# A fused attention-and-MLP kernel rewritten in hand order: q grouped by head, the gate as a column of K, attention gated apart, W3's remainder in column tiles

## The chip, the cores and the metric

The kernel runs on one core of a Trainium2 chip. The time is the device time of one execution, in microseconds (us). "Fast" runs are those in the undisturbed state; every run quoted here is fast, except one single run whose state is unknown and which is marked. TensorE is called PE in the profile, VectorE is DVE, ScalarE is ACT, GpSimd is POOL, and SP is the engine that issues most of the DMA transfers. PEld is the loading of weights into PE, which overlaps with matmuls.

## The reference, cut to what matters

The inputs are bf16: x is 2048 by 640, there are 32 heads of 20 features, and the MLP is 1728 wide.

```
q, k, v = split(x @ wqkv)                 # A: linear attention
phi = where(t > 0, t + 1, exp(t)) + 1e-6
kv  = sum_s phi(k)[s,d] v[s,e]            # per head, 20 x 20
z   = sum_s phi(k)[s,d]                   # per head, 20
a   = ((phi(q) @ kv) / (phi(q) @ z + 1e-6)) @ wo

h   = gelu(layernorm(x) @ w1)             # B: mixer
hs  = (h in four groups of 160 features, shifted by +1, -1, +2, -2 tokens) @ w2
x1  = x + hs
b   = x1 + gelu(layernorm(x1) @ w3) @ w4

g   = sigmoid(sum(x * gate_w))            # one number per token
out = g * a + (1 - g) * b
```

## The kernel before

Tokens come in 16 chunks of 128 or 4 tiles of 512, and features in 5 chunks of 128. kv is never built from v: G = x^T phi(k) is, then kv = wv^T G, and M = kv @ wo, so that attention costs five matmuls per half of an output chunk. A tile framework orders the instructions of each engine by priority. PSUM, where the matmuls write, is handed out as four "pairs" (`pp`), each 128 x 2 x 512 in float32. An engine that still has to read a pair keeps PE from writing into it.

The stages on PE are, in order: K, Q (with the gate), G, then W1 with kv and W2 for the first tile, then four rounds. A round holds W3 of a tile with W2 of the next one, then W4 and the attention product. The parts that the change and the argument touch:

```
    def gate_unit():                      # gate: 5 tiny + 20 column-tiled matmuls
        ...
            nc.tensor.matmul(pt[:, 1, 32 * dc:32 * (dc + 1)], lhsT=gw_row[0:1, ...], rhs=ones32[0:1, :], ...)
        ...
                nc.tensor.matmul(pt[32 * t:32 * (t + 1), 0, :], lhsT=gwb[:, dc, :], rhs=xT[:, dc, ...], ...)

    def z_unit():                         # called after the last G
        ... 32 column-tiled sums over phi(k) ...
        nc.vector.tensor_copy(zv[:, 0], pt[:, :, 0:HD])                            # zz, high part
        nc.vector.tensor_tensor(zv[:, 1], pt[:, :, 0:HD], zv[:, 0], op=ALU.subtract)  # zz, low part
        nc.sync.dma_start_transpose(zT[:], zz[:])
        nc.vector.tensor_reduce(zc[:], zT[:]..., op=ALU.add)                       # needs the transpose
        for j in range(DC):
            nc.vector.tensor_scalar_mul(zbd[:, j, :], hmask[:, j, :], zc[:, j:j + 1])

    def kv_unit(gs):                      # called with (0,1), (2,3), (4,5): three pairs
        pt = pair()
        ... 5 matmuls for each of the six blocks of kv ...
                    nc.vector.tensor_tensor(kvT[0:w, b, ...], pt[0:w, i, ...], mask[...], op=ALU.mult)

    def scale_unit(j, i):                 # 10 times: expand r = g/den to chunk j, scale phi(q)
        pt = pair()
        for t in (2 * i, 2 * i + 1):
            nc.tensor.matmul(pt[:, t % 2, :], lhsT=emat[32 * t:32 * (t + 1), j * P:(j + 1) * P], rhs=r_bf[...], ...)
        nc.vector.tensor_tensor(sl, sl, pt[:], op=ALU.mult)

    def w1_unit(t, fcs):
        ...
                for g in range(4):        # chunk 4 holds the last 32 features of each shift group
                    nc.scalar.activation(hsT[32 * g:32 * (g + 1), 4, o:o + TS], pt[32 * g:32 * (g + 1), i, :],
                                         ACT.Gelu_apprx_tanh)

    def w3_unit(t, fcs):                  # F = 1728 is padded to 14 chunks of 128: the last one is half zeros
        ...
```

## Time and profile before

| kernel before | |
|---|---|
| median of 3 runs | 288.09 us (287.43 to 288.32) |
| span in the profile | 286.1 us |
| PE, DVE, ACT busy | 273.3 us (96%), 132.6 (46%), 92.0 (32%) |

These lines are from the profile page: the busy times, the PE row and the granted PE clock in 40 equal slices (a digit is tenths), the share of each engine in the chain of work that ended last, and the costliest group.

```profile
span 286.1 us, 4181 instructions
PE 273.3 (96%) x1730; PEld 162.2 (57%) x1730; DVE 132.6 (46%) x266; ACT 92.0 (32%) x117; POOL 24.1 (8%) x47
...
PE   6999999999967999999899999999999999999994
...
PEclk9999999999985999999999999999999999999999
...
PE 78%; DVE 8%; DMA 6%; ACT 3%; issue 2%; POOL 1%; DVEq 0%; SPq 0%; ACTq 0%; POOLq 0%
...
L450 PE MATMUL pp<-lnxT,w_sb 128*128 128x512 bf16 x280 | 63.4, 379 | 1.2 <-ACT h_1268 L452 0.8
```

PE is the bound, but the slices twelve and thirteen (about 80 to 93 us) show it at six and seven tenths, and its clock at eight and five tenths. The mean of one matmul in a group (379 ns) overlaps with its neighbours; in a stream ten such 512-column matmuls take 2.16 us, 216 ns each. Next is the table of windows over the stages as PE's order gives them (K, then, after a cut, G, W1 and round 0). The columns are: window, length; busy time of PE, PEld, DVE, ACT and POOL with instructions in brackets; granted clock; DMA share; GB/s.

```profile
0.00:28.80 28.80, 26.25 (x174) 17.58 (x175) 17.74 (x35) 11.85 (x16) 10.15 (x24) 1.00 1.00 276
...
52.15:75.18 23.03, 23.03 (x193) 16.32 (x192) 18.81 (x57) 4.59 (x8) 3.81 (x6) 1.00 0.30 59
75.18:114.45 39.27, 34.19 (x195) 17.13 (x191) 20.93 (x54) 18.86 (x32) 5.08 (x7) 0.87 0.51 115
114.45:164.04 49.59, 48.34 (x304) 28.00 (x303) 25.37 (x36) 17.23 (x22) 1.27 (x2) 1.00 0.10 24
```

The stage from 75.18 us loses time twice: 39.27 − 34.19 = 5.1 us of idle time, and a clock of 0.87. Round 0 is 8.4 us longer than round 1, which takes 41.16 us without a gap. A finer table of windows of the same kernel, same columns, shows where the clock drops, and the waits of PE between 70 and 120 us (total us, times, longest) say for what.

```profile
80.00:85.00 5.00, 2.69 (x27) 2.11 (x26) 2.47 (x5) 3.15 (x6) 0.00 (x0) 0.85 0.24 46
85.00:90.00 5.00, 2.76 (x15) 1.22 (x14) 2.66 (x17) 0.00 (x0) 2.55 (x3) 0.50 0.74 148
90.00:95.00 5.00, 5.00 (x16) 1.94 (x15) 0.00 (x0) 1.09 (x2) 0.00 (x0) 0.63 1.04 368
```

```profile
PE pp L285 <- DVE zz L261: 2.3, 1, 2.3
PE pp L358 <- DVE kvT L293: 2.2, 1, 2.2
```

VectorE's own order in time in this stretch (start us, busy us, line, operation, and the idle time before it with its releaser) says why it was late:

```profile
86.41 0.22 DVE L263 TENSOR_REDUCE zc<-zT 128x5 f32<-128x40 bf16 x1 [3.50 <-DMA zT<-zz]
...
87.36 1.39 DVE L293 TENSOR_TENSOR kvT<-pp,bmask 120x120 bf16<-120x120 f32 x10
```

VectorE takes its instructions in order. It came to `zz`, the z sums, only at 81.24 us, behind rows of layer norm 1, and the first kv pair waited for it (2.3 us). Then it stood at `zc`, which needs the transpose of z, for 3.50 us, and the masking of kv (`kvT`), which needs nothing from z, stood behind it. The three kv pairs stayed full, and PE had no pair to write W1 into.

### The profile page before, as it was taken

The page shows a single profiled execution, that of the slowest core. Times are in us where ns is not written, and L with a number is a line of the kernel's source. Part 1 is how long each engine was busy: PE and PEld are TensorE (multiplying, and loading weights), DVE is VectorE, ACT ScalarE, POOL GpSimd, SP SyncE. Part 2 cuts the span into 40 slices and gives each one's busy share as a digit, 9 for nine tenths or more (in the row PEclk, how much of TensorE's full clock was granted, in tenths as well). Part 3 has the DMA queues.
Part 4 walks back from the last instruction along what each step waited for, and adds up shares of the span by engine and source line. Part 5 has one row for each costly group of instructions (what it writes and reads, how often), then busy time and mean ns, then how long its engine had stood idle before and what let it go on. Part 6 is the DMA issues. An engine that isn't in the chain of part 4 may idle for free.

```text
span 286.1 us, 4181 instructions
## 1 busy us (share of the span) xinstructions
PE 273.3 (96%) x1730; PEld 162.2 (57%) x1730; DVE 132.6 (46%) x266; ACT 92.0 (32%) x117; POOL 24.1 (8%) x47
## 2 busy tenths in 40 slices
PE   6999999999967999999899999999999999999994
PEld 3677444677542543544377655577655577545772
DVE  1588788888733367485625244034252045100121
ACT  1455435311440529732314022404033304143000
POOL 8500100011213010000001000001000010000000
PEclk9999999999985999999999999999999999999999
DMA  8999884025548804000002400003300007100001
GB/s 207 214 318 363 221 269 136 3 40 98 109 79 231 170 0 92 2 0 0 0 2 66 98 23 0 2 23 69 92 2 0 2 23 112 51 0 0 25 32 37
DMA packets 43464, 22.96 MB, mean 80 GB/s; under 512 B 33670, under 2 KB 42375, under 8 KB 43447
## 3 DMA queue, kind: packets, MB, share of 16 engines
q1 hardware_dynamic: 41669, 19.68, 28.1%
q0 software_dynamic: 464, 2.21, 2.3%
q10 hardware_dynamic: 1314, 0.82, 0.9%
q8 instruction: 13, 0.21, 0.3%
q14 instruction: 4, 0.03, 0.0%
HBM read 11.96 MB, written 2.62 MB: 51 GB/s over the span
## 4 chain that ended last, share of the span: by engine, by line
PE 78%; DVE 8%; DMA 6%; ACT 3%; issue 2%; POOL 1%; DVEq 0%; SPq 0%; ACTq 0%; POOLq 0%
PE pp L450 21%; PE pp L463 21%; PE pp L202 8%; PE pp L460 8%; PE pp L212 7%; PE pp L419 6%; DMA lnxT<-ln 4%; PE pp L358 3%; DMA x_sb<-in_A_x_dram 1%; DMA zT<-zz 1%; DVE st1s L185 1%; DVE ln L347 1%; POOL rstd_191 L182 1%; PE pp L303 1%; ACT ln L437 1%
## 5 line engine op out<-in xcount | busy, mean ns | idle before, releaser
L450 PE MATMUL pp<-lnxT,w_sb 128*128 128x512 bf16 x280 | 63.4, 379 | 1.2 <-ACT h_1268 L452 0.8
L450 PEld LDWEIGHTS <-w_sb 128*128 128x128 bf16 x280 | 27.1, 98 | 32.3 <-issue 2.5
L192 ACT ACTIVATE e<-pp 128x640 bf16<-128x640 f32 (+2 forms) x28 | 21.8, 780 | 24.0 <-PE pp L202 14.8
L460 PE MATMUL pp<-m_sb,pqT 128*128 128x320 bf16 x160 | 27.0, 299 | 0.0
L419 PE MATMUL pp<-w_sb,hsT 128*128 128x320 bf16 x160 | 23.9, 299 | 0.0
L202 PE MATMUL pp<-wkq,xT 128*128 128x320 bf16 x160 | 23.1, 308 | 0.0
L358 PE MATMUL pp<-lnxT,w_sb 128*128 128x512 bf16 x80 | 20.8, 422 | 2.2 <-DVE kvT L293 2.2
L212 PE MATMUL pp<-xT,wkq 128*128 128x512 bf16 x100 | 22.1, 379 | 0.0
L273 PE MATMUL pp<-pk,x_sb 128*128 128x320 bf16 x160 | 21.9, 299 | 0.0
L419 PEld LDWEIGHTS <-hsT 128*128 128x128 bf16 x160 | 15.4, 98 | 8.1 <-issue 0.7
L202 PEld LDWEIGHTS <-xT 128*128 128x128 bf16 x160 | 16.1, 101 | 6.7
L460 PEld LDWEIGHTS <-pqT 128*128 128x128 bf16 x160 | 15.7, 98 | 6.7
L273 PEld LDWEIGHTS <-x_sb 128*128 128x128 bf16 x160 | 15.7, 98 | 6.2
L463 PE MATMUL pp<-w_sb,h_1682 128*128 128x320 bf16 x112 | 16.5, 299 | 0.0
L463 PE MATMUL pp<-w_sb,h_2026 128*128 128x320 bf16 x112 | 16.5, 299 | 0.0
L463 PE MATMUL pp<-w_sb,h_2370 128*128 128x320 bf16 x112 | 16.5, 299 | 0.0
L463 PE MATMUL pp<-w_sb,h_1268 128*128 128x320 bf16 x112 | 16.5, 299 | 0.0
L212 PEld LDWEIGHTS <-wkq 128*128 128x128 bf16 x100 | 9.6, 98 | 11.6 <-issue 0.4
L358 PEld LDWEIGHTS <-w_sb 128*128 128x128 bf16 x80 | 8.3, 107 | 13.8 <-issue 4.5
L326 DVE TENSOR_TENSOR pqT<-pqT,pp 128x1024 bf16<-128x1024 bf16 x10 | 12.1, 1217 | 6.4 <-PE pp L323 6.3
L366 ACT ACTIVATE hsT<-pp 128x512 bf16<-128x512 f32 x16 | 8.6, 596 | 18.8 <-PE pp L358 18.8
L194 DVE SCALAR_TENSOR_TENSOR pk<-pp,e 128x640 bf16<-128x640 f32 x16 | 13.2, 825 | 1.7
(197 smaller groups left out, 280.7 us busy)
## 6 DMA issues: line engine op xcount, KB each, us to landing
out_dram<-oc SPq DMA_DIRECT2D x15, 160.0 KB, 2.0
w_sb<-in_B_w_dram SPq DMA_DIRECT2D x1, 2160.0 KB
w_sb<-in_B_w_dram POOLq DMA_DIRECT2D x1, 2080.0 KB, 11.0
x_sb<-in_A_x_dram SPq DMA_DIRECT2D x3, 640.0 KB, 8.5
wkq<-in_A_wqkv_dram SPq DMA_DIRECT2D x2, 800.0 KB, 9.8
wkq<-in_A_wqkv_dram ACTq DMA_DIRECT2D x2, 400.0 KB, 4.8
w_sb<-in_B_w_dram SPq DMA_DIRECT2D x1, 800.0 KB
wo_sb<-in_A_wo_dram SPq DMA_DIRECT2D x5, 150.0 KB, 9.3
```

What stands on the lines that cost most here:

```text
L192: nc.scalar.activation(ev, src, ACT.Exp)
L194: nc.vector.scalar_tensor_tensor(dst, src, 0.0, ev, op0=ALU.max, op1=ALU.add)
L202: nc.tensor.matmul(pt[:, hf, 0:c1 - c0], lhsT=xT[:, dc, cs], rhs=wk_sb[:, dc, c0:c1], start=(dc == 0), stop=(dc == DC - 1))
L212: nc.tensor.matmul(pt[:, i, :], lhsT=wq_sb[:, dc, j * P:(j + 1) * P], rhs=xT[:, dc, ts_], start=(dc == 0), stop=(dc == DC - 1))
L273: nc.tensor.matmul(pt[:, hf, 0:HD], lhsT=x_sb[:, c, fc * P:(fc + 1) * P], rhs=pk[:, c, hf * HD:(hf + 1) * HD], start=(c == 0), stop=(c == ...
L326: nc.vector.tensor_tensor(sl, sl, pt[:], op=ALU.mult)
L358: nc.tensor.matmul(pt[:, i, :], lhsT=w1_sb[:, dc, CG * fc:CG * fc + P], rhs=lnxT[t][:, dc, :], start=(dc == 0), stop=(dc == DC - 1))
L366: nc.scalar.activation(hsT[:, fc, o:o + TS], pt[:, i, :], ACT.Gelu_apprx_tanh)
L419: nc.tensor.matmul(pt[:, hf, 0:HD], lhsT=hsT[:, fc, 2 + c * P:2 + (c + 1) * P], rhs=w2_sb[:, fc, hf * HD:(hf + 1) * HD], start=(fc == 0), ...
L450: nc.tensor.matmul(pt[:, i, :], lhsT=w3_sb[:, dc, fc * P:(fc + 1) * P], rhs=lnT[:, dc, :], start=(dc == 0), stop=(dc == DC - 1))
L460: nc.tensor.matmul(pt[:, hf, 0:HD], lhsT=pqT[:, j, c * P:(c + 1) * P], rhs=m_sb[:, j, hf * HD:(hf + 1) * HD], start=(j == 0), stop=False)
L463: nc.tensor.matmul(pt[:, hf, 0:HD], lhsT=h2[:, fc, cc * P:(cc + 1) * P], rhs=w4_sb[:, fc, hf * HD:(hf + 1) * HD], start=False, stop=(fc == ...
```

## The change

The intent: less PE work, and an order in which PE never waits for a late z. The scheduler is switched off (`manual_schedule`), so each engine runs its instructions as written. The diff is long; this is its core, with cuts marked.

```
+    ctx.enter_context(tc.manual_schedule())
 # q regrouped by head: every chunk j holds 4 of the 20 features of all 32 heads
+        nc.gpsimd.tensor_copy(wq_sb[:, dc, :]...("p (j h i) -> p j h i"), wq_raw[:, dc, :]...("p (h j i) -> p j h i"))
 # so one expansion of r serves all five chunks
-    def scale_unit(j, i): ...                               # 20 matmuls, 10 multiplies from PSUM
+    def r_unit():                                           # 4 matmuls, 2 copies
+    def scale_t(t):                                         # 4 multiplies of 128 x 2560
+        nc.vector.tensor_tensor(sl, sl, rb[:, t:t + 1, :].broadcast_to([P, DC, TS]), op=ALU.mult)
 # the gate is column 641 of K
-    def gate_unit(): ...
+        gq.dma_start(wk_sb[:, :, D:D + 1], gate_w.rearrange("(c p o) -> p c o", p=P, o=1))
+                n = HD + hf                                 # in k_mm: second half has 321 columns
 # K starts on the chunks of wk as they land; z within Q
+    k_mm(kp[0], 0, (0,))
+    x_turn(1)
+    k_mm(kp[0], 0, (1,))
+    ...
+        if n == 1:
+            zp = z_mm()
+        if n == 2:
+            z_evac(zp)
 # all six kv blocks in one pair, M in 32-column tiles
-    kv_unit((0, 1)); kv_unit((2, 3)); kv_unit((4, 5))
+    kv_unit()
+                    nc.tensor.matmul(pt[32 * q:32 * (q + 1), hf, 0:HD], lhsT=kvT[:, 2 * q + p, j, :], ...)
 # one gelu for chunk 4, four copies on VectorE; layer norm 2 on VectorE, scaling of x1 on ScalarE
+                nc.scalar.activation(hx[:, 0:TS], pt[:, i, :], ACT.Gelu_apprx_tanh)
+                for g in range(4):
+                    nc.vector.tensor_copy(hsT[32 * g:32 * (g + 1), 4, o:o + TS], hx[32 * g:32 * (g + 1), 0:TS])
 # attention gated apart from W4, in units of its own between those of W3
+    def att_unit(t, cc):                                    # x1 += gate * (phi(q) @ M)
 # W3's last 64 features: two 64-column tiles of 256 tokens each, in place of 512 columns of half zeros
+                        nc.tensor.matmul(pt[FR * v:FR * (v + 1), k, 0:LT], lhsT=w3_sb[:, dc, FF * P:F],
+                                         rhs=lnT[:, dc, v * LT:(v + 1) * LT], ...)
-    for fcs in w1_split: ... den_unit() ... scale_unit(i - 1, 0) ... m_unit(i)   # den with W1, the rest in round 0
+    g_unit(0); z_fin(); dp = den_mm(); ... r_unit()                              # within G
+    for j in range(DC): m_unit(j)                                                # before W2
```

## The prediction

> **What bounds the kernel now.** TensorE: the page gives PE 96% busy, VectorE 46%, ScalarE 32%; the chain that ended last is 78% PE. In the chain a 512-column matmul streams in 216 ns (30 in 6.47 us), a 320-column one in 136 ns. The last three W3/W4 rounds take 41.2, 41.2 and 35.8 us without a gap; the first takes 49.5 us (114.5 to 164.0), because the r expansions, the M products and short waits sit in it.
>
> The weak stretch is 80 to 95 us (table of windows): PE busy 2.69 and 2.76 us in two 5 us windows, waiting for VectorE (zz 2.3 us, kvT 2.2 us), granted clock 0.85, 0.50, 0.63. So 4.6 us idle and, estimated from the clocks, some 5 us lost at half speed. The Trainium skill (TensorE: Matmul & The Clock Gate, Part 1) says an idle window of about 3.4 us halves the clock; this dip agrees.
>
> **PE work.**
> - r expansion, 20 to 4 matmuls: before, about 0.64 us in each of five W3 steps, now about 0.5 us once: -2.8 us.
> - Gate: 20 column-tiled and 5 tiny matmuls go; a 641st column of K costs nothing: -1.4 us.
> - W3: 280 to 260 full matmuls, plus 40 of 256 columns in two 64-column tiles: -4.3 + 2.2 = -2.1 us. The Trainium skill (TensorEngine Tiling, Theoretical Speedup) promises up to 2x; the trace supports it: 32-column z sums, 32 in 1.27 us (40 ns against 136).
> - M in 32-column tiles, 80 at about 40 ns instead of 20 at 136: +0.5 us.
> - The rest is unchanged. Attention gated apart adds no matmul; it costs 16 VectorE operations of about 0.88 us, in rounds where VectorE is a third busy.
> Sum: -6 us.
>
> **What it moves.** z comes during Q, so its transpose (3.5 us) is done long before W1; kv and M no longer wait for it. That should remove most idle time and the clock dip at 80 to 95 us: -7 to -9 us. The fourfold 32-partition gelu (589 ns each) becomes one ScalarE pass plus copies, which removes gaps of 1 us near 113 us. K starts on chunks of wk as they land: 0 to -1 us.
>
> **New costs.** VectorE is nearly as loaded as PE in the G/W1 stretch: 16 statistics at 1.12 us, a 3.4 us reciprocal, scales and LN, about 28 us against PE's 24 us of G. I expect M to wait for kvT about 1 us. The gate column is a transfer of 640 two-byte pieces that the second K matmul waits for (0 to 1.5 us). The regrouping of wq on GpSimd should finish (24 us) before Q starts (28 us).
>
> **Sum.** Q starts near 28 us (29 before), G near 51 (52), round 0 near 108 (114.5); rounds 40.7, 40.7, 40.7, 35.2 us; tail 3.9. Span about 269, time about 2 us more, and 1 us for waits not foreseen: 272 us, 5.6% less, range 267.5 to 278. Chances: faster by over 2% 0.95, within 2% 0.04, slower 0.01.
>
> **What would show it.** Right: round 0 about 41 us, rounds 1 and 2 half a microsecond shorter, granted clock 1.00 from 75 to 110 us, M's wait under 2 us. Wrong: PE waiting for kvT or hsT near 85 to 95 us with a clock dip (adds 5 us); PE waiting on the gate column at 4 to 7 us or on wq at 28 us; column-tiled W3 not running two at a time (rounds of 41.2 or more).
>
> **What would make it wrong.** VectorE falling behind in the G/W1 stretch: in hand order one late operation delays all behind it.

## The result and the profile after

The kernel took 274.23 us (median of 4 runs, 273.93 to 274.57), against 287.89 us (median of 4 runs, 287.43 to 288.32: the three above and one more) before. The ratio is 0.9518, with a 95% interval of 0.95 to 0.9537. Ratios and intervals are from fast runs alone; they are not quite the ratios of the medians (0.9526 here). The prediction was 272.0 us with a range of 267.5 to 278.

The profile page after, the lines that answer to those of before:

```profile
span 272.4 us, 4350 instructions
PE 264.0 (97%) x1781; PEld 160.3 (59%) x1781; DVE 141.1 (52%) x275; ACT 84.5 (31%) x124; POOL 29.0 (11%) x65
...
PEclk9799999999999999999999999999999999999998
...
PE 94%; DMA 2%; ACT 1%; issue 1%; DVE 0%; ACTq 0%; POOLq 0%
```

The dip of the clock near 85 us has gone and a smaller one has appeared in the second slice. The chain that ended last is now 94% PE, and 2% is one DMA transfer. The stages after (table of windows, columns as before; again K, G, W1 and round 0):

```profile
0.00:32.32 32.32, 27.81 (x187) 18.45 (x188) 17.63 (x34) 12.62 (x31) 9.47 (x32) 0.95 0.98 260
...
55.21:78.68 23.47, 23.47 (x186) 16.03 (x185) 22.64 (x59) 6.21 (x8) 4.06 (x6) 1.00 0.26 43
78.68:110.73 32.05, 31.54 (x252) 17.18 (x250) 25.64 (x60) 15.10 (x26) 10.46 (x17) 1.00 0.64 145
110.73:151.78 41.05, 41.05 (x269) 25.64 (x268) 16.88 (x31) 13.38 (x17) 1.28 (x2) 1.00 0.12 29
```

| stage | before | after | difference |
|---|---|---|---|
| head and K | 28.94 | 32.32 | +3.4 |
| Q | 23.21 | 22.89 | −0.3 |
| G | 23.03 | 23.47 | +0.4 |
| W1, kv, first W2 | 39.27 | 32.05 | −7.2 |
| round 0 | 49.59 | 41.05 | −8.5 |
| rounds 1, 2, 3 | 41.16, 41.20, 35.80 | 40.88, 40.88, 35.46 | −0.9 |
| tail | 3.9 | 3.4 | −0.5 |
| span | 286.1 | 272.4 | −13.7 |

The table starts Q at its first matmul, 28.94 us in the kernel before; the windows further up cut 0.14 us ahead of it. Nearly the whole gain is in the W1 stage and in round 0, and the head gives 3.4 us of it back. G is longer by what moved into it: the denominator (1.26 us) and r (0.40 us) came, the z sums (1.27 us) went to Q. The same finer windows as before, now with a clock of 1.00 throughout (the sum of PE's idle time in these 15 us is 0.5 us):

```profile
80.00:85.00 5.00, 5.00 (x38) 2.76 (x37) 3.97 (x9) 1.28 (x1) 2.85 (x4) 1.00 0.66 131
85.00:90.00 5.00, 4.49 (x34) 2.34 (x32) 2.23 (x8) 3.64 (x7) 3.64 (x7) 1.00 0.34 52
90.00:95.00 5.00, 5.00 (x93) 3.03 (x91) 4.61 (x14) 4.24 (x8) 0.00 (x0) 1.00 0.99 365
```

The W1 stage adds up from these views: 4.6 us of idle time went; the second W1 and kv, which ran at about half clock before, took 7.33 and 2.65 us and now take 4.48 and 1.60 us, so 3.9 us; the denominator (1.26 us) moved into G; and M moved in, for 2.9 us. That is −6.9 us, where −7.2 was measured.

In round 0, a few pieces of the chain of work before, in order of time (start, us, what), show what the r expansions cost; the last two are from round 1, which has none:

```profile
123.16 0.32 PE pp L323 x2
123.48 2.26 PE pp L450 x10
125.75 0.32 PE pp L323 x2
126.07 1.47 PE pp L419 x10
...
135.58 0.32 PE pp L323 x2
135.90 0.98 PE pp L303 x4
...
164.04 2.16 PE pp L450 x10
166.19 1.36 PE pp L419 x10
```

Each pair of r matmuls (L323), 32 rows of PE wide, took 0.32 us. The last two pairs ran as four matmuls at once, as PE's order in time of the same kernel shows:

```profile
139.89 0.39 PE L323 MATMUL pp<-r_bf,emat 32*128 32x512 bf16 x4
```

So the ten pairs took nine such slots, 2.9 us. The full matmuls right after a pair took longer too: ten of W3 2.26 in place of 2.16 us, ten of W2 1.47 in place of 1.36 us. Six groups show this, 0.65 us in all. The five M units took 3.2 us, four of 0.54 or 0.55 us and the last of 0.98 us, where weights of 120 and of 40 rows take turns; they moved to the stage before. With 1.25 us of idle time (49.59 − 48.34), about 0.3 us by which the W3 groups behind the two waits were longer, and 0.3 us for the column tiles, this adds up to 8.6 us, where 8.5 was measured.

The head is where the prediction missed. PE's order in time after, from 5 us, and the wait that goes with it:

```profile
5.40 0.30 PE L199 MATMUL pp<-wk_sb,xT 128*128 128x320 bf16 x1
7.71 0.30 PE L199 MATMUL pp<-wk_sb,xT 128*128 128x321 bf16 x1 [2.01 <-DMA wk_sb<-in_gate_w_dram]
```

The list of DMA issues of that kernel in the first 8 us (what, issuing engine, kind, count, KB, us from issue to landing) has the transfer:

```profile
wk_sb<-in_gate_w_dram POOLq DMA_DIRECT2D x1, 1.2 KB, 6.4
```

The second K matmul is the first with 321 columns, and it waited 2.01 us for the gate column: 1.2 KB in 640 pieces of two bytes, 6.4 us from issue to landing. This trace records the full clock from 4.76 to 8.18 us and half of it from 8.18 to 11.59 us, as the next two windows of the same kernel show. In the second of them PE gets through 11 matmuls in 2 us, where it gets through 17 at full speed (one that straddles an edge counts in both windows).

```profile
8.00:10.00 2.00, 1.94 (x17) 1.36 (x15) 0.68 (x2) 0.00 (x0) 1.37 (x3) 0.54 1.14 227
10.00:12.00 2.00, 2.00 (x11) 1.18 (x9) 0.30 (x1) 0.00 (x0) 0.00 (x0) 0.60 1.03 220
```

### The profile page after: what moved, and what is told of

It is laid out like the page before. It is cut to its first block, busy times and chain, and to the rows that moved or that the text cites. A ratio compares the mean times of both kernels' runs of the same rounds, so it can differ in the third digit from the quotient of the medians.

```text
span 272.4 us, 4350 instructions
## 1 busy us (share of the span) xinstructions
PE 264.0 (97%) x1781; PEld 160.3 (59%) x1781; DVE 141.1 (52%) x275; ACT 84.5 (31%) x124; POOL 29.0 (11%) x65
## 4 chain that ended last, share of the span: by engine, by line
PE 94%; DMA 2%; ACT 1%; issue 1%; DVE 0%; ACTq 0%; POOLq 0%
PE pp L524 22%; PE pp L499 21%; PE pp L347 8%; PE pp L452 8%; PE pp L377 8%; PE pp L483 8%; PE pp L246 8%; PE pp L199 8%; DMA wk_sb<-in_gate_w_dram 2%; PE pp L415 1%; PE pp L504 1%; ACT e L191 1%; PE pp L262 0%; PE pp L285 0%; PE pp L215 0%
## 5 line engine op out<-in xcount | busy, mean ns | idle before, releaser
L524 PE MATMUL pp<-w_sb,h 128*128 128x320 bf16 x448 | 61.5, 299 | 0.0
L507 ACT ACTIVATE h<-pp 128x1024 bf16<-128x1024 f32 (+1 forms) x28 | 27.8, 993 | 103.8 <-PE pp L499 95.5
L524 PEld LDWEIGHTS <-h 128*128 128x128 bf16 x448 | 43.5, 98 | 17.5 <-issue 0.8
L499 PEld LDWEIGHTS <-w_sb 128*128 128x128 bf16 x260 | 25.4, 98 | 26.7
L530 DVE SCALAR_TENSOR_TENSOR oc<-pp,omg,x 128x640 bf16<-128x640 f32 x15 | 13.3, 884 | 44.7 <-PE pp L524 44.7
L486 DVE SCALAR_TENSOR_TENSOR x<-pp,gate,x 128x640 f32<-128x640 f32 x16 | 13.9, 868 | 29.4 <-PE pp L483 29.4
L199 PE MATMUL pp<-wk_sb,xT 128*128 128x320 bf16 (+1 forms) x160 | 23.9, 309 | 2.4 <-DMA wk_sb<-in_gate_w_dram 2.0
L455 DVE TENSOR_TENSOR x<-pp,x_sb 128x640 f32<-128x640 f32 x16 | 13.1, 820 | 23.4 <-PE pp L452 23.4
L191 ACT ACTIVATE e<-pp 128x640 bf16<-128x640 f32 (+1 forms) x26 | 21.2, 830 | 9.3 <-PE pp L246 7.9
L246 PE MATMUL pp<-xT,wq_sb 128*128 128x512 bf16 x100 | 21.9, 379 | 0.0
```

The costliest lines, as they stand in the source:

```text
L191: nc.scalar.activation(ev, src, ACT.Exp)
L199: nc.tensor.matmul(pt[:, hf, 0:n], lhsT=xT[:, dc, c * P:(c + 1) * P], rhs=wk_sb[:, dc, hf * HD:hf * HD + n], start=(dc == 0), stop=(dc == ...
L246: nc.tensor.matmul(pt[:, t % 2, :], lhsT=wq_sb[:, dc, j * P:(j + 1) * P], rhs=xT[:, dc, t * TS:(t + 1) * TS], start=(dc == 0), stop=(dc == ...
L486: nc.vector.scalar_tensor_tensor(x1, pt[:, :, 0:HD], gate[:, c:c + 1], x1, op0=ALU.mult, op1=ALU.add)
L499: nc.tensor.matmul(pt[:, k, :], lhsT=w3_sb[:, dc, fc * P:(fc + 1) * P], rhs=lnT[:, dc, :], start=(dc == 0), stop=(dc == DC - 1))
L507: nc.scalar.activation(h2[:, 2 * i * TS:2 * i * TS + n], pt[:].rearrange("p h e -> p (h e)")[:, 0:n], ACT.Gelu_apprx_tanh)
```

## The experiments

Twelve kernels ran. Each call of runs shared one chip and the runs of the kernel before on it. The medians of the kernel before were 286.59 (7 runs; e1 to e4), 287.7 (7; e10, e12, e6), 287.34 (11; e14, e9, e13, e11) and 287.81 us (7; e5). All results were correct except e2.

### Theories

On the head, the theory was that the gate column's wait and the cold clock behind it cost the time. The rivals were that the K matmuls interleaved over chunks of wk cost it, or that the clock's warm-up merely fell differently in these runs. On the middle, the theory was that the early z alone removes the waits and the dip. The rival was that the single kv pair, or the shorter work of ScalarE, is needed as well. On the rounds, the question was what the column tiles are worth.

### e1, e2, e3: the gate column

e1_gate_row loads the gate weights as five rows of 128 and turns them into the column with one small PE transpose. e2_gate_zero sets the column to zero, with no transfer at all (wrong: relative error 0.0318). e3_row_serial is e1 with K's first three chunks computed one after the other.

```
-        gq.dma_start(wk_sb[:, :, D:D + 1], gate_w.rearrange("(c p o) -> p c o", p=P, o=1))
+    sp.dma_start(gw5[:], gate_w.rearrange("(c p) -> c p", p=P))                                     # e1, e3
+    nc.tensor.transpose(warm[...][:, D:D + DC], gw5[:], ident[0:DC, 0:DC])                          # e1, e3
+    nc.vector.tensor_copy(wk_sb[:, :, D:D + 1], warm[...][:, D:D + DC]...)                          # e1, e3
+    nc.vector.memset(wk_sb[:, :, D:D + 1], 0.0)                                                     # e2 in its place
-    k_mm(kp[0], 0, (0,)); x_turn(1); k_mm(kp[0], 0, (1,)); ...                                      # e3
+    x_turn(1); k_mm(kp[0], 0, range(DC)); k_evac(kp[0], 0); ...                                     # e3
```

> Theory A (the gate column's 640 two-byte pieces cost the head): the column comes as five contiguous rows and one PE transpose; no wait of 2.0 us on it, no cold clock at 7.7 to 12 us, Q starts near 29 us instead of 32.4, time 270.5 to 271.5 us. Theory B (the interleaved start with chunks of wk, three turns through one PSUM bank and three evacuations in a burst costs the head): Q still near 31 to 32 us, time 273 us or more.

> Wrong result on purpose: the gate column is set to zero by VectorE, no transfer at all. Theory A: the upper bound of what the column can give back, within 0.5 us of the row version (270.5 to 271.5 us). Theory B: 273 us or more.

> Gate row as in the first run, and K's first three chunks one after the other instead of interleaved by chunk of wk. Theory A: within 0.7 us of the row version, either way. Theory B: over 1.5 us faster than the row version.

| kernel | us, median (range, runs) | ratio to before (95%) | Q starts at |
|---|---|---|---|
| e1_gate_row | 272.36 (270.94 to 273.17, 4) | 0.9499 (0.9438 to 0.9559) | 30.22 |
| e2_gate_zero | 272.74 (272.5 to 273.66, 4) | 0.9523 (0.9468 to 0.9578) | 30.79 |
| e3_row_serial | 272.71 (272.5 to 272.91, 4) | 0.9514 (0.9451 to 0.9576) | 31.17 |

The times of e1 and e2 lie above the 270.5 to 271.5 us expected if the gate column is to blame and below the 273 us of the rival, so they settle nothing. In all three the wait of 2.01 us is gone from the profile and Q starts 1.1 to 2.1 us sooner than in the changed kernel (32.32). The row of the gate costs no more than no gate at all. The order of the K matmuls makes no difference that these runs can show, which speaks against the rival of the interleaving. But the ratios alone do not show a gain over the changed kernel, whose ratio was 0.9518: it did not run on this chip. So this comparison was repeated on one chip, in e9 and e14 below.

### e4: the early z alone, in the kernel before

```
         for js in q_split:
             q_unit(t, js)
+        if t == 0:
+            z_unit()
...
     for fc in range(DC):
         g_unit(fc)
-    z_unit()
```

> The kernel before with one call moved: z's sums during Q instead of after G. If the idle time and the clock dip at 80 to 95 us came from VectorE standing in order behind z's transpose: PE idle there under 1 us, granted clock 1.00, 279 to 282 us (7 to 9 us less than before). Rival (the wait for kvT and the dip come from VectorE's normalization work, z only stands in the same place): under 3 us less, dip still there.

This failed: 290.65 us (287.89 to 291.48, 4 runs), ratio 1.0125 (1.0051 to 1.02), slower than the kernel before, though by less than 2%. The VectorE and PE lines of e4 in order of time say why, and the last line is a window of e4 (columns as before):

```profile
46.90 0.22 DVE L263 TENSOR_REDUCE zc<-zT 128x5 f32<-128x40 bf16 x1 [5.45 <-DMA zT<-zz]
```

```profile
49.73 2.29 PE L212 MATMUL pp<-xT,wkq 128*128 128x512 bf16 x5 [5.42 <-DVE pqT L194]
```

```profile
90.00:95.00 5.00, 2.35 (x21) 1.29 (x20) 3.55 (x14) 1.47 (x3) 3.33 (x4) 1.00 0.58 120
```

The wait that stood in front of W1 had moved into Q. VectorE stood for 5.45 us at the same reduction, in order, with Q's phi behind it; the wait for the transpose was longer there than before W1 (3.50 us). PE then stood for 5.42 us and its clock was 0.58 from 50 to 55 us. The wait for kvT (2.65 us) was still there, but the dip of the clock was not: it was granted 1.00 from 54.2 us on, through that wait. Moving a producer earlier is worth nothing if its consumer moves with it.

### e10: the early z split, its use held back

Here the z sums and the transpose are issued in Q, and the reduction comes after the last phi, in G. The copy from pqT only ties the reduction to that point.

```
         nc.sync.dma_start_transpose(zT[:], zz[:])
+        return zT
+
+    def z_fin(zT):
+        nc.vector.tensor_copy(zc[:], pqT[:, DC - 1, S - DC:S])
         nc.vector.tensor_reduce(zc[:], ...)
...
+        if t == 0:
+            zT = z_unit()
...
         g_unit(fc)
-    z_unit()
+        if fc == 0:
+            z_fin(zT)
```

The transposed gate values also moved to another buffer, so that the two transposes do not share one.

> The kernel before with z's sums during Q, and VectorE's use of the transposed sums held back until after the last phi of Q (by one 5-column copy), so that nothing in Q stands behind the transpose. If the stall of the last run in Q (5.4 us and a cold clock) was VectorE waiting in order for z's transpose: no gap in Q, G starts near 52 to 53.5 us instead of 61.8, and G to the first W3 takes 55 to 56 us (62.3 in the kernel before), time 281 to 283 us. If moving z is no gain by itself: 286 us or more. A wait for kvT of 2 to 3 us near 82 us should remain, since it came with z early too.

It took 285.1 us (283.73 to 286.56, 4 runs), ratio 0.992 (0.9851 to 0.9989): a part of the gain expected (281 to 283 us). Q was not quite free of gaps: PE waited 0.79 us for a phi there. In its profile G starts at 53.25 and W3 at 110.91 us, which is 57.7 us for that stretch against 62.3 before, 1.27 of them being the z sums themselves. What was left is mainly one wait, shown by this line of PE's order in time in e10:

```profile
85.54 6.18 PE L362 MATMUL pp<-lnxT,w_sb 128*128 128x512 bf16 x19 [3.40 <-DVE kvT L297]
```

kvT was still late, now behind layer-norm rows on VectorE, and PE still waited for a pair; the trace has the clock at half from 86.59 to 90.0 us. The early z alone does not explain the gain.

### e11: the split z, and all six kv blocks in one pair

A first attempt to give the layer-norm rows a fourth buffer in place of this did not fit into SBUF (label e11_z_split_work4: the build failed, 4.8 kB were left and 6 were needed), so it ran on no chip and the place of those rows stays untested.

> As the last, with four buffers instead of three for the normalized rows that the transposes read. If the wait for kvT that is left comes from VectorE held up by these transposes (three buffers): wait under 1 us, no clock dip, 277 to 279 us. Rival (VectorE is short of time there): wait within 0.5 us of the last run's, time the same.

```
-                nc.tensor.matmul(pt[0:gw[g], i, 0:gw[g]], ...)
+                nc.tensor.matmul(pt[0:gw[g], g // 3, (g % 3) * GW:(g % 3) * GW + gw[g]], ...)
-    kv_unit((0, 1)); kv_unit((2, 3)); kv_unit((4, 5))
+    kv_unit(range(6))
```

> The kernel before with z's sums in Q and their use held back, and the six kv blocks in one PSUM pair instead of three, as in the changed kernel. If the 3.4 us wait for kvT that was left is W1's second round waiting for PSUM pairs that VectorE has not yet emptied: wait under 0.5 us, no cold stretch near 86 us, G to the first W3 in 52 to 54 us (57.7 with three pairs), time 280 to 281.5 us. Rival (VectorE's lateness holds up W1 by its normalized rows, whatever the pairs): G to the first W3 57 us or more, 284 us or more.

It took 283.13 us (282.65 to 283.7, 4 runs), ratio 0.9859 (0.9815 to 0.9904). The masking of kv starts on VectorE at 85.34 us, which is 0.4 us later than in e10 (84.97), but PE does not wait for it any more: W1 goes on at 82.27 us and the clock is 1.00 in every window from 75 to 95 us. So it is not the lateness of kvT that cost PE the time, but the three pairs that it kept. G to W3 took 55.6 us, against 57.7 in e10 and 55.5 in the changed kernel. The expectation was 52 to 54, and 280 to 281.5 us for the time; a new wait made up the difference, shown by PE's order in time and ScalarE's in e11:

```profile
104.60 2.32 PE L362 MATMUL pp<-lnxT,w_sb 128*128 128x512 bf16 x10 [2.40 <-ACT hsT L370]
107.90 1.24 PE L365 MATMUL pp<-lnxT,w1x 128*128 128x512 bf16 x5 [0.98 <-ACT hsT L374]
```

```profile
101.04 2.54 ACT L442 ACTIVATE ln<-x,nb,rstd 128x640 bf16<-128x640 f32 x3 [4.41 <-DVE nb L437]
103.49 1.05 ACT L370 ACTIVATE hsT<-pp 128x512 bf16<-128x512 f32 x2
...
105.47 2.38 ACT L374 ACTIVATE hsT<-pp 32x512 bf16<-32x512 f32 x4
```

ScalarE does the rows of layer norm 2 and the fourfold gelu (2.38 us) in order, and PE waited 3.4 us for them. The changed kernel has layer norm 2 on VectorE and a single gelu, and has no such wait.

These stretches do not hold the same work. That of the kernel before has the z sums in it (1.3 us), and that of the changed kernel has M (2.9 us) and r (0.4 us). Less these, G to W3 takes 61.0 us before, 57.7 in e10, 55.6 in e11 and 52.2 in the changed kernel. So the split z brings 3.4 us, the single pair 2.1 us, and the rest 3.4 us, as much as PE waited for ScalarE in e11. That last step is read off the traces and not tested apart: hand order as such, with the scheduler off, is in it too.

### e6: the fourfold gelu put back into the changed kernel

```
-                nc.scalar.activation(hx[:, 0:TS], pt[:, i, :], ACT.Gelu_apprx_tanh)
-                for g in range(4):
-                    nc.vector.tensor_copy(hsT[32 * g:32 * (g + 1), 4, o:o + TS], hx[32 * g:32 * (g + 1), 0:TS])
+                for g in range(4):
+                    nc.scalar.activation(hsT[32 * g:32 * (g + 1), 4, o:o + TS], pt[32 * g:32 * (g + 1), i, :], ...)
```

> The changed kernel with the four 32-partition gelu operations of before in place of one pass and four copies. If that part matters: waits of PE on hsT in the W1 stretch grow from 0.5 us to 1.5 us or more, and G to the first W3 takes 56.5 us or more (55.5 in the changed kernel). If ScalarE has the room in hand order: within 0.3 us.

This was one look: 276.54 us, a single run of unknown state. Its head was 1.3 us slower than that of the changed kernel (Q at 33.62 against 32.32), though the code of the head is the same, so only the stretch behind it is read. G to W3 took 56.6 us against 55.5, which is 1.1 us, and M waited for ScalarE, a wait that the changed kernel does not have. So in this order the single gelu is worth about 1 us, and layer norm 2, the other work taken from ScalarE, was not tried apart.

### e14, e9, e12, e13: the head again, on one chip, with more rounds

e14_after_again is the changed kernel, unedited. e9_row_edges is e1 with the two small memsets of the edges of hsT (L419, L420) moved up in GpSimd's order. e12_before_head is e1 with the head of the kernel before: wk in two transfers, two chunks turned by PE, and K chunk by chunk. e13_head_edges is e12 with the edges moved as in e9.

```
     nc.gpsimd.memset(hsT[:, :, 0:4], 0.0)              # e9, e13: moved ahead of the w1x copies,
     nc.gpsimd.memset(hsT[:, :, S:S + 4], 0.0)          # from behind the rstd operations of layer norm 1
...
-    for dc in range(DC):
-        aq.dma_start(wk_sb[:, dc, 0:D], A_wqkv[dc * P:(dc + 1) * P, D:2 * D])                       # e12, e13
+    aq.dma_start(wk_sb[:, :, 0:HD], wqkv_v[:, :, D:D + HD])
+    aq.dma_start(wk_sb[:, :, HD:D], wqkv_v[:, :, D + HD:2 * D])
...
+    for c in range(NCH):
+        pt = pair()
+        k_mm(pt, c)
+        k_evac(pt, c)
```

> The changed kernel with the whole head of the kernel before (wk in two halves, two chunks turned by PE each in its own PSUM pair, K chunk by chunk, the two halves of a chunk one after the other) and the gate column as a row with a PE transpose. If the interleaved start is what the gate row version still loses (Q at 30.2 us against 28.9 before): Q starts at 28.8 to 29.5 us, time 0.7 to 1.5 us under the gate row version, near 271. Rival (the extra column or the evacuation's extra copy slows K): Q at 30 us or later.

> The changed kernel itself, for a comparison on one chip with the two that follow: 273 to 275 us.

> The changed kernel with the gate column as a row and a PE transpose, and GpSimd's memset of hsT's edges moved ahead of the LN work (ScalarE's first gelu waited 2.7 us for it and PE 0.5 + 0.4 us in turn). If the gate column costs its 2 us wait on average: 1.5 to 3 us under the changed kernel of the same rounds. Rival (the moment at which the clock warms wanders by some us from run to run and hides most of it): under 1.5 us. The edges: PE's wait on hsT near 86 us gone, 0.5 to 0.9 us.

> As the last, with the head of the kernel before. If the interleaved start loses something: 0.7 to 1.5 us under the last. Rival (only the warm-up of the clock differs): within 0.7 us of the last on average.

| kernel | us, median (range, runs) | ratio to before (95%) | Q starts at |
|---|---|---|---|
| e14_after_again | 275.05 (274.05 to 275.52, 6) | 0.9569 (0.9538 to 0.9601) | 32.2 |
| e9_row_edges | 272.55 (270.31 to 272.63, 6) | 0.947 (0.9434 to 0.9506) | 31.48 |
| e13_head_edges | 271.33 (269.88 to 272.56, 6) | 0.9434 (0.9396 to 0.9472) | 30.32 |
| e12_before_head (another chip) | 272.54 (270.96 to 273.73, 4) | 0.9472 (0.9417 to 0.9528) | 31.52 |

e12 missed its expectation (Q at 28.8 to 29.5 us); its clock, below, says why. e14, e9 and e13 ran on one chip. e9 is 2.5 us below e14, and their intervals do not overlap. About 0.5 us of that is the wait of PE for hsT near 86 us, which e9's profile does not have. So the gate column costs about 2 us. This is an estimate, since e9 makes both edits at once, but it agrees with the wait of 2.0 us that the profiles of the changed kernel and of e14 show. e13 is another 1.2 us lower in the median, but its interval overlaps with that of e9, so the gain from the old head is probable and not settled. e13 beats both kernels: it is 5.7% faster than the kernel before and 1.4% faster than the changed one.

The wait near 86 us came from GpSimd. Its lines and one of VectorE, in the changed kernel, in order of time:

```profile
77.05 1.08 POOL L319 TENSOR_TENSOR rstd<-rstd,mhalf 128x4 f32<-128x4 f32 x1
...
82.45 2.48 POOL L319 TENSOR_TENSOR rstd<-rstd,mhalf 128x4 f32<-128x4 f32 x1
```

```profile
82.56 1.48 DVE L304 TENSOR_TENSOR pqT<-pqT,rb 128x2560 bf16<-128x2560 bf16 x1
```

The same four-column power took 2.48 us in place of 1.08 while VectorE multiplied two SBUF tiles for 1.48 us, and the memset behind it (L419, at 84.90 us), which ScalarE's gelu had to wait for, was late. The Trainium skill (SBUF — State Buffer, Who interferes with whom) says that a VectorE instruction with two SBUF inputs contends with a GpSimd instruction that reads SBUF. This trace agrees: the extra time, 1.40 us, is close to the length of the multiplication. In e9 and e13 the power was as slow (2.48 and 2.61 us), but with the memset ahead of it PE waited for nothing there.

The rival of the warm-up is true as well, and the traces let its part be taken off. A K matmul starts 0.136 us after the one before at full clock and 0.267 us at half. In the kernels with exactly the head of before, the full clock begins at 4.67 us, ahead of K (e10), at 8.40 (before), 8.33 (e11) and 9.81 us (e4), and Q starts at 27.78, 28.94, 28.93 and 29.57 us. With the changed head K gets it for good at 11.59 (the changed kernel), 11.47 (e14), 11.21 (e5) and 13.77 us (e6), and Q starts between 32.2 and 33.6 us. Half of the time that PE worked at half clock after K's first matmul is lost. By this estimate the loss is 0 to 1.9 us in the first four profiles and 1.7 to 3.2 us in the second four. Less the loss, Q starts at 27.6 to 27.8 us in the first four and at 30.4 to 30.6 us in the second. In e1, e2, e3 and e9 it is 28.7 to 29.3 us, and in e12 and e13 28.6 to 28.8 us.

So the gate column costs 1 to 2 us whatever the clock does. The old order of the head gives back 0.3 us (e12 against e1) to 0.4 us (e13 against e9), although PE waits in it for the gate row, which was loaded behind wk, for 0.7 us in e12 and 0.9 us in e13. Those waits are most of what these two still have over the kernel before; a row that comes sooner was not tried. The clock itself is no worse for the wait: e9, which has no such wait, was at half until 10.93 us and lost 2.5 us by it, against 1.7 us in the changed kernel and 1.2 us in the kernel before. A single raw profile places Q no better than to 1 us or so, and the timed rounds decide about the total. The windows of e12 and then of e10 (columns as before) show how the column of the clock can mislead here:

```profile
8.00:10.00 2.00, 2.00 (x10) 1.10 (x8) 0.00 (x0) 0.08 (x2) 0.00 (x0) 1.00 1.01 228
10.00:12.00 2.00, 2.00 (x9) 1.14 (x8) 1.15 (x2) 0.69 (x2) 0.00 (x0) 1.00 1.19 224
13.00:15.00 2.00, 2.00 (x17) 1.46 (x15) 1.34 (x3) 1.13 (x3) 0.00 (x0) 1.00 1.03 195
```

```profile
8.00:10.00 2.00, 2.00 (x17) 1.43 (x16) 1.47 (x3) 1.02 (x2) 1.87 (x4) 1.00 1.02 232
```

PE is busy throughout, with K's matmuls of 320 columns or one more, and does 9 or 10 of them in 2 us in e12 where it does 17 in e10. The granted clock reads 1.00 in all of these windows. But the trace of e12 has no record of the clock before 12.54 us, and the view prints 1.00 where it has none; from 12.6 us on the matmuls of e12 are 0.136 us apart. The Trainium skill (TensorE: Matmul & The Clock Gate, Part 1) says that the moment of warm-up depends on a free-running window and varies from run to run. These runs agree: the last change to full clock before Q came between 4.67 us (e10) and 13.77 us (e6), and the records of the changed kernel (4.76, 8.18 and 11.59 us) lie 3.41 us apart.

### e5: W3's last 64 features padded again, in the changed kernel

```
-    w3_sb = const.tile([P, DC, F], BF16)
+    w3_sb = const.tile([P, DC, (FF + 1) * P], BF16)    # last 64 columns zero
...
-            if fc < FF:
+            if fc <= FF:                                # 5 full matmuls in place of 10 in column tiles
```

> The changed kernel with W3's last 64 features padded to a full 128-column tile again, as in the kernel before: five 512-column matmuls (5 x 216 ns = 1.08 us) in place of ten 256-column ones in two column tiles (0.67 us in the changed kernel). If the two tiles run side by side and nothing else holds the rounds: the second and third round 41.3 us (40.9 in the changed kernel), 0.41 us longer in each of four, 1.6 us in all, so 275.5 to 277 us. Rival (a wait sets the rounds): rounds within 0.1 us of 40.9.

It took 276.11 us (275.49 to 276.83, 4 runs), ratio 0.9614 (0.954 to 0.9688). The rounds of its profile tell more than the times, which carry the head's scatter: rounds 1 and 2 took 41.19 us each, against 40.88. So the column tiles save 0.3 us a round, 1.2 us in all. By themselves they save 0.41 us: ten column-tiled matmuls of 256 columns take 0.67 us in the chain of work (L504), five full ones 1.08 us. The other 0.11 us turns up right behind them: W4's 112 matmuls in the first round take 15.32 us in the changed kernel and 15.21 us in e5. The full matmuls behind each r expansion lost the same 0.11 us in the kernel before.

## Why the prediction was right or wrong

The total was right: 274.23 us in a range of 267.5 to 278, 2.2 us above the point. In part this was luck. Against its stages the head was 4.3 us longer, G to W3 1.5 us shorter, the four rounds 1.0 us longer in all and the tail 0.5 us shorter, and a reserve of 1 us for waits not foreseen took up some of the rest.

- **The moves, "-7 to -9 us": right in size, incomplete in its reason.** The idle time (4.6 us) and the half-speed time (3.9 us) are both gone, 8.5 us together. But the prediction credited the early z alone, and tied the dip to an idle window of about 3.4 us. The longest wait ahead of the dip was 2.31 us, and in e4 PE waited 2.65 us in the same place at a clock of 1.00, so how long a wait halves the clock is not shown here. e4 also shows that z moved early with its consumer makes the kernel slower. e10 shows that the split z leaves a wait of 3.40 us for kvT. e11 shows that the single kv pair removes that wait, and that ScalarE then needs less work before the stretch is as short as in the changed kernel. The change has all of these together: the split z, the single pair, layer norm 2 on VectorE and the single gelu. What each step brings is worked out under e11.
- **"M to wait for kvT about 1 us" did not come.** With one pair for kv, W1's second tile ran between kv and M, and the masks (1.28 us) were done by then. G to W3 took 55.5 us where the prediction had 57.
- **"Q starts near 28 us" is the step that failed: it started at 32.3.** The prediction named the wait for the gate column (0 to 1.5 us), yet put a net gain into the sum. It was 2.01 us. The half clock until 11.59 us cost about 1.7 us more, but some such loss comes with every head here except e10's (1.2 us in the kernel before), so the wait cannot be called its cause. e9 against e14 puts the gate column at about 2 us. e13 suggests 1.2 us (medians) for the new order of the head, not settled; with the clock's part taken off it is 0.4 us, and e13 still waits 0.9 us for the gate row.
- **r expansion "-2.8 us": close, by two errors.** It counted ten slots, and there were nine (2.9 us); it left out the 0.65 us lost by the full matmuls behind them. For 0.4 us now that makes −3.1 us.
- **W3 "-2.1 us": less.** e5 gives −1.2 us. The column tiles were sized at 55 ns a matmul, took 67, and 0.11 us a round was given back in W4. So rounds 1 and 2 took 40.88 us, not 40.7; the sign given for a failure ("rounds of 41.2 or more") was not met.
- **M "+0.5 us": it was −0.3 us.** It went from 3.2 us to 2.90 us (80 matmuls, 36 ns each); the prediction took the last of the five old units for as short as the others. The gate's "-1.4 us" was −1.6 us in Q (23.21 us less 100 full matmuls at 216 ns), where the z sums took 1.3 us of it back: Q is 0.3 us shorter.
- **"VectorE falling behind", the named risk, did not happen.** VectorE was nearly full in G (22.64 of 23.47 us), and yet PE waited there for nothing; but one order of GpSimd and VectorE did cost 0.5 us near 86 us.

## What to carry to other kernels

When an engine works in order, look at what its late operation holds in PSUM, not only at how late it is: kvT was as late in e11 as in e10, and PE lost nothing once it held one pair in place of three. Move a producer early, but leave its consumer where its input is surely ready. A small transfer that the first matmuls need can hold up the whole head. Where the warm-up scatters by microseconds, compare heads by timed rounds on one chip, or take the time at half clock off each profile first, by the spacing of the matmuls.

## What the Trainium skill lacked or had wrong

- TensorE: Matmul & The Clock Gate, Part 1, warns in "Seeing it yourself" that the clock's records can be unreliable. Here they agreed with the matmuls wherever there were any: in e12 the first record of the full clock is at 12.54 us, and the matmuls' spacing falls from 0.267 to 0.136 us at 12.6 us. What misled was the time ahead of a trace's first record, which our view prints as 1.00; I found no page that says so. The same part lets work run at half clock for its first 3.4 us or so. In e12 PE worked at half clock without a break for longer, from 7.03 to 12.54 us, which is 5.5 us.
- TensorEngine Tiling (Array Packing), Key Properties, says that a change of tiling mode drains TensorE, without a number: here the full matmuls right behind such tiles took 0.11 us longer, for 32-row tiles and 64-column tiles alike, and the old M unit that alternates 120 and 40 rows took 0.24 us a matmul in place of 0.135; whether that is the drain was not tested. Its "up to 2x" for 64 columns came to 1.6x (0.67 us for what 5 full matmuls do in 1.08 us), or 1.4x with the 0.11 us; its "up to 4x" for 32 columns to 3.8x (36 ns a matmul in M against 136 ns).
- DMA: Bandwidth & Descriptors, Anatomy of one DMA, fits 2.0 us plus bytes for a transfer issued from GpSimd, so 2.0 us for 1.2 KB. In 640 two-byte pieces it took 6.4 us to land. The page says that small descriptors are slow, but its fit has no term for the number of pieces. How much of the 6.4 us they cost is not shown: the five transfers of 160 KB issued in the same 8 us took 5.0 us (median) to land.
- I found no page that says that what PE loses to a late consumer can hang on the number of PSUM buffers that it holds; e10 and e11 show it (a wait of 3.40 us with three pairs against none with one, with the masks 0.4 us later).
